# Block-sparse attention with a mixture of experts: score matmuls that read neighbouring and outer key blocks straight from the keys' tile

## The chip, the cores and the metric

The kernel runs on one core of a Trainium2 chip, with float32 data. The metric is the device time of one execution in microseconds (us), and the median of the runs counts. TensorE (PE) does the matmuls, VectorE (DVE) reductions and transposes, ScalarE (ACT) exponentials and copies, GpSimd (POOL) copies, and SyncE (SP) issues DMAs. SBUF is the on-chip memory that all of them read, PSUM the memory that matmuls write.

## The reference, cut to what matters

Attention over 4 batches of 8 heads, 768 positions of 64 features, in 24 blocks of 32 positions. A query block sees its own block, its two neighbours, blocks 0 and 23, and three sampled blocks; query blocks 0 and 23 see all. The result goes through a layer of 8 experts with 4 slots each.

```python
scores = scale * np.matmul(q, k.transpose(0, 1, 3, 2))
mask = np.abs(blk_i - blk_j) <= window            # window = 1
mask = mask | (blk_i == 0) | (blk_j == 0) | (blk_i == n_blocks - 1) | (blk_j == n_blocks - 1)
for qb in range(n_blocks):
    for kb in sampled_blocks[qb]:
        mask[qb * block:(qb + 1) * block, kb * block:(kb + 1) * block] = True
...
attn = np.exp(scores - np.max(scores, axis=-1, keepdims=True))
attn = attn / (np.sum(attn, axis=-1, keepdims=True) + 1e-09)
out = np.matmul(attn, v)
...
logits = x @ phi      # x: (3072, 512), phi: (512, 32)
# slots: softmax of logits over the rows, times x; two expert layers w1, w2; combine: softmax over the slots
```

## The kernel before, in words

**Layout.** For a batch, the keys lie in one tile, `ktile`, transposed: 128 partitions are two heads of 64 features each, then 4 such head pairs, then 768 positions. Queries lie the same way in `q`, loaded for two query blocks at a time and scaled. One score matmul takes 64 partitions (one head) of 32 queries as weights and streams key columns past them; its output is a 32-partition strip of a PSUM tile `s` of 2 query blocks by 256 columns. So 8 tiles of TensorE's array (2 halves of rows, 4 strips of columns) work at a time.

**A pair of query blocks** is `plan_pair` (L502). A batch has 11 pairs for blocks 1 to 22, and the dense blocks 0 and 23 apart (`plan_dense`, L700). For each of the pair's two blocks, `stage_k` (L429) collects the 8 visible key blocks side by side in a staging tile `kst` of 256 columns, one of four that take turns: `fixed` (L437) copies the three neighbours (L442) and, when the staging tile is new to this batch, blocks 0 and 23 (L440), on GpSimd; `sampled_` (L444) copies the three sampled blocks, on ScalarE (L448) or GpSimd (L450), at addresses read from a register. Then `qk` (L515) runs 2 x 4 x 2 = 16 matmuls of 256 columns (L521). VectorE takes the maximum (L538), ScalarE the exponential (L543), VectorE transposes 32 by 32 (L550). The value products (L615) take the transposed chunks as weights, and the values of sampled blocks from a staging tile `vrs` that GpSimd fills (L466). Chunk numbers, which are the column blocks of the scores, stand in `av_heads` (L628 and L653).

**Order.** A planner (`Plan`, L80) sets the order of each engine's instructions before the program runs: each task has engines that may run it with an estimated duration (`("PE", 1.08)` for the score matmuls), tasks that it depends on, rotating buffers that it takes, and a due time (`n`, the pair's number, plus an offset). Among tasks that could start about the same time on an engine, the one with the least `turn` goes first. `turn` is the due time plus an entry of a table that is indexed by the order in which the kinds of task, told apart by their function's first line, were first added:

```python
kind = self.kinds.setdefault(f.__code__.co_firstlineno, len(self.kinds))
t.turn = key + BEHIND.get(kind, 0.0)
BEHIND = {17: 1.1, 23: -2.5, 24: 2.8, 37: -1.2, 46: 1.0, 70: 1.8, 71: -1.2}
```

`fixed` is kind 19, `sampled_` 20, the pair's score matmuls 21, maxima 22, exponentials 23, transposes 24, value staging 25. Kind 17 is the dense rows' exponential; 37 copies transposed rows out, 38 is the gate's logits, 46 the slot sums, 47 their accumulation; 70 normalises the combine weights, 71 and 72 split them in two terms.

**Weights.** 64 tiles of 512 KB. `NPRE` of them go into tiles of their own during attention, 12 into buffers that the last batch leaves free, and at the end of attention 9 more into the last batch's keys' and values' buffers, and `NLB` into the room that the staging tiles leave, plus 2 (`LORD`, L59, is the order of the last two groups). The rest are loaded when a used tile is free.

Of the kernel before, what the change touches and what calls it, by code (L numbers as in the profile page):

```python
# [11 lines left out]
F32 = mybir.dt.float32  # L12
I32 = mybir.dt.int32
F32R = mybir.dt.float32r
AF = mybir.ActivationFunctionType
# [5 lines left out]
BLK, NB, NR = 32, 24, 3  # L21
P = 128
NP = 4
# [14 lines left out]
NKST, NVR, NQ = 4, 6, 4  # L38
# [13 lines left out]
EH = NE // PW  # L52
OG = 4 // PW
TG = 512 // CW
NPRE, NLB = 11, 10
KW = {"ktile": 3, "v0": 6, "v1": 6, "ptd": 3}


LORD = [0, 1, 2, 3, 4, 5, -1, -2, -3, -4, 6, 7, 8, 9, -5, -6, 10, 11]  # L59
LCOLS = [slice(c, c + LC) for c in range(0, WP, LC)]  # L60
H1, HALF = 3, 4
CPES = [0, 0, 3, 3, 3, 2, 0, 0]
# [17 lines left out]
class Plan:  # L80
# [6 lines left out]
    def add(self, f, opts, deps, key, acq=(), byte=0, pre=None, pace=False):  # L87
        t = Task(f, opts if isinstance(opts, list) else [opts], deps, key, acq, byte, pre, pace)
        kind = self.kinds.setdefault(f.__code__.co_firstlineno, len(self.kinds))
        t.turn = key + BEHIND.get(kind, 0.0)  # L90
        self.tasks.append(t)
        return t
# [96 lines left out]
def attn_moe_kernel(ctx, tc, qT, kT, vfull, vtab, sampled, phi, w1, w2, out):  # L189
# [107 lines left out]
    pst = att.enter_context(tc.tile_pool(name="pst", bufs=1))  # L297
# [1 line left out]
    ktile, vtile = [None] * B, [None] * B  # L299

    ptd = [ptdb[:, r * NB * 2 * BLK:(r + 1) * NB * 2 * BLK].rearrange("p (k j q) -> p k j q", k=NB, j=2) for r in range(2)]
    kst = [pst.tile([P, NP, 256], F32, name=f"kst{n}") for n in range(NKST)]
    qst = [pst.tile([P, NP, 2, BLK], F32, name=f"q{n}") for n in range(NQ)]

    vrs = [None] * NVR
# [77 lines left out]
    use = []  # L383
# [40 lines left out]
        v_use[b].append(t_v[b])  # L424


    fresh, nst, nvs = {}, [0], [0]

    def stage_k(b, i, n, use):  # L429
        k = nst[0] % NKST  # L430
        nst[0] += 1
        st, new = kst[k], fresh.get(k) != b
        fresh[k] = b

        w, r0 = (0, 96) if i % 2 else (32, 0)

        def fixed(t):  # L437
            kv = ktile[b]
            if new:
                POOL.tensor_copy(out=st[:, :, 128:192].rearrange("p c (g s) -> p c g s", g=2),  # L440
                                 in_=kv.rearrange("p c (g s) -> p c g s", g=NB)[:, :, 0:NB:NB - 1, :])
            POOL.tensor_copy(out=st[:, :, w:w + 96], in_=kv[:, :, (i - 1) * BLK:(i + 2) * BLK])  # L442

        def sampled_(t):  # L444
            for j, o in enumerate((r0, 192, 224)):
                src = ktile[b][:, :, ds(t.vals[j] * BLK, BLK)]
                if t.eng == "ACT":
                    ACT.activation(out=st[:, :, o:o + BLK], in_=src, func=AF.Copy, scale=1.0)  # L448
                else:
                    POOL.tensor_copy(out=st[:, :, o:o + BLK], in_=src)  # L450

        f = add(fixed, ("POOL", 0.82 if new else 0.47), [t_k[b]], n - 4, acq=[("kst", use)])
        r = add(sampled_, [("ACT", 0.62), ("POOL", 0.73)], [f, t_sreg], n - 2.5,
                pre=lambda e: block_numbers(sreg, i, e, NB - 1))
        k_use[b].extend([f, r])
        use.extend([f, r])
        return st, r

    def stage_v(b, i, n, use):
# [42 lines left out]
    def plan_pair(b, g, n):  # L502
        T = tile_of(b, (g + 1) // 2)
        w = 1 if g and g % 2 == 0 else 0
        u = Rec()
        u.g = g
        kd, ku = [], []
        for r in range(2):
            use = []
            kd.append(stage_k(b, 2 * g + 1 + r, n, use))  # L510
            ku.append(use)
        t_q, q_use = plan_q(u, b, g + 1, n)
        s_use = [[], []]

        def qk(t):  # L515
            u.s = [psA.tile([P, 2, 256], F32, tag="s", name="s", bufs=SB) for _ in range(2)]
            for j in range(2):
                for p in range(NP):
                    for r in range(2):
                        s_ = slice(64 * r, 64 * r + 64)  # L520
                        PE.matmul(u.s[r][32 * p:32 * p + 32, j, :], lhsT=u.q[s_, p, j, :],  # L521
                                  rhs=kd[j][0][s_, p, :], start=True, stop=True)

        t_qk = add(qk, ("PE", 1.08), [t_q] + [k for _, k in kd], n, acq=[("s", s_use[0]), ("s", s_use[1])])
        qks[n] = t_qk
        q_use.append(t_qk)
        for use in ku:
            use.append(t_qk)
        u.p = [None] * 2
        if not T.turned:  # L530
            T.pt = [None] * 2
            T.n_pt = nt[0]
            nt[0] += 2
        for r in range(2):
            def top(t, r=r):
                u.nm = getattr(u, "nm", {})
                u.nm[r] = pw.tile([P, 2], F32, tag="nm", name="nm", bufs=4)
                DVE.tensor_reduce(out=u.nm[r], in_=u.s[r], axis=AX.X, op=ALU.max, negate=True)  # L538

            def exp(t, r, j):  # L540
                if j == 0:
                    u.p[r] = pw.tile([P, 2, 256], F32, tag="p", name="p", bufs=PB)
                ACT.activation(out=u.p[r][:, j, :], in_=u.s[r][:, j, :], func=AF.Exp,  # L543
                               bias=u.nm[r][:, j:j + 1], scale=1.0)


            def turn(t, r=r):
                if w == 0:
                    T.pt[r] = pw.tile([P, 8, 4, BLK], F32, tag=f"ptt{(T.n_pt + r) % PTB}", name="ptt", bufs=1)
                DVE.transpose(out=T.pt[r][:, :, 2 * w:2 * w + 2, :].rearrange("p k j q -> p j k q"),  # L550
                              in_=u.p[r].rearrange("p j (k q) -> p j k q", k=8))

            t_m = add(top, ("DVE", 0.6), [t_qk], n + 0.1 + 0.01 * r)
            p_use = []
            t_e = []
            for j in range(2):
                t_e.append(add(lambda t, r=r, j=j, exp=exp: exp(t, r, j), ("ACT", 0.37), [t_m] + t_e, n + 0.2 + 0.01 * r,
                               acq=[("p", p_use)] if j == 0 else []))
            s_use[r].append(t_e[1])
            acq = []  # L560
            if w == 0:
                T.pt_use = getattr(T, "pt_use", {})
                T.pt_use[r] = []
                acq = [("ptt", T.pt_use[r])]
            t_t = add(turn, ("DVE", 0.64), [t_e[1]] + ([T.turned[r]] if w else []), n + 0.3 + 0.01 * r, acq=acq)
            p_use.append(t_t)
            T.turned.append(t_t)
        u.vst = []
        for r in range(2):
            use = []  # L570
            v, t_s = stage_v(b, 2 * g + 1 + r, n, use)
            u.vst.append(v)
            T.staged.append(t_s)
            T.use.append(use)
        T.units.append(u)
        if g == 0 or w:
            plan_av(T, n)
# [45 lines left out]
    def av_heads(T, rs_):  # L623

        vt, us = vtile[T.b], T.units
        one = len(us) == 1
        m = 64 * len(us)
        for n, c in enumerate((4, 5)):  # L628
            for r in rs_:
                for g, s_ in G2:  # L630
                    av_mm(T.av, 64 * r if one else 0, m, g, r, T.pt[r][s_, c, 0:m // BLK].rearrange("p j q -> p (j q)"),
                          vt[s_, :, VPOS((0, NB - 1)[n]), r, :], n == 0, False)
        for c in (1, 2):
            for w, u in enumerate(us):
                for r in rs_:
                    for g, s_ in G2:
                        av_mm(T.av, 64 * r if one else 64 * w, 64, g, r,
                              T.pt[r][s_, c, 2 * w:2 * w + 2].rearrange("p j q -> p (j q)"),
                              vt[s_, :, VPOS(2 * u.g + c), r, :], False, False)
        for n in range(NR + 1):  # L640
            for w, u in enumerate(us):
                for r in rs_:
                    for j in range(2):
                        i = 2 * u.g + 1 + j
                        for g, s_ in G2:
                            if n == 0:

                                k, c = (i - 1, 0) if j == 0 else (i + 1, 3)
                                if k in (0, NB - 1):
                                    continue  # L650
                                v_ = vt[s_, :, VPOS(k), r, :]
                            else:
                                c = ((3, 0)[j], 6, 7)[n - 1]  # L653
                                v_ = u.vst[j][s_, :, n - 1, r, :]
                            av_mm(T.av, (64 * r if one else 64 * w) + 32 * j, 32, g, r, T.pt[r][s_, c, 2 * w + j], v_,
                                  False, n == NR)
# [778 lines left out]
```

## Time and profile before

| | |
|---|---|
| median of 3 runs | 312.58 us (310.84 to 313.65) |
| span of the profiled execution, first to last instruction | 312.2 us |
| time of the profiled execution beyond its span | not recorded; the median is 0.4 us above the span |
| TensorE busy | 278.2 us, 7167 matmul passes and as many weight loads |
| VectorE, ScalarE, GpSimd busy | 216.2, 162.1, 185.2 us |
| mean granted TensorE clock | 0.979 |
| DMA | 63.62 MB, 204 GB/s over the span |

A float32 matmul is two passes in the profile, each with its weight load. The profile has a row for each group of instructions: line, engine, operation, the tiles written and read, count, busy time of the group, mean duration of one in ns, idle time of the engine just before them, and what ended most of that idle time. "issue" there means that the engine waited for nothing that the profile shows. PEld is TensorE's weight loading, which overlaps its matmuls. Instructions are themselves fetched by DMA, in queues of the kind "instruction".

### The profile page before, as it was taken

What the parts mean: (1) busy time and instruction counts of PE and PEld (TensorE: products, weight loads), DVE (VectorE), ACT (ScalarE), POOL (GpSimd) and SP (SyncE); (2) the same over time, 40 slices, a digit from 0 to 9 for tenths busy, and PEclk for the clock granted to TensorE, in tenths of its full rate; (3) what the DMA queues carried; (4) which work ended last, traced back from release to release, by engine and by line L of the source; (5) the groups of instructions that cost most, each with busy time, mean ns of one, the idle gap of its engine ahead of it and who ended that gap; (6) DMA issues with size and microseconds to landing.
All of it is one profiled execution on the core that took longest, in us unless ns stands there. A gap on an engine that the chain in (4) does not pass through costs nothing.

```text
span 312.2 us, 17614 instructions
## 1 busy us (share of the span) xinstructions
PE 278.2 (89%) x7167; PEld 191.7 (61%) x7167; DVE 216.2 (69%) x499; ACT 162.1 (52%) x492; POOL 185.2 (59%) x521
## 2 busy tenths in 40 slices
PE   7689888759999999999999999999999889999750
PEld 6148656536787666777677776877577763466340
DVE  4789967536899879789998778999897253103260
ACT  0766748443367867737667763866761241004250
POOL 2879499772667869958599994847958004000000
PEclk9899999997999999999999999999999999999996
DMA  7935766540045654024475511667779999999998
GB/s 246 399 115 161 208 192 195 152 115 4 19 146 168 196 168 143 7 74 146 138 199 150 141 37 56 154 186 220 207 206 298 354 367 363 413 406 405 391 335 271
DMA packets 33506, 63.62 MB, mean 204 GB/s; under 512 B 5521, under 2 KB 18962, under 8 KB 33426
## 3 DMA queue, kind: packets, MB, share of 16 engines
q1 hardware_dynamic: 33280, 62.37, 62.1%
q8 instruction: 56, 0.92, 1.3%
q14 instruction: 24, 0.20, 0.2%
q10 hardware_dynamic: 146, 0.13, 0.1%
HBM read 56.19 MB, written 6.29 MB: 200 GB/s over the span
## 4 chain that ended last, share of the span: by engine, by line
PE 55%; DVE 14%; DMA 12%; issue 5%; POOL 4%; POOLq 4%; ACT 2%; SPq 1%; ACTq 0%; DVEq 0%
PE av L615 22%; PE s L521 6%; DMA q<-in_qT_dram 5%; PE avd L615 5%; PE pf L1233 5%; PE sd L717 3%; PE pso L1241 3%; DMA w<-in_w_dram 3%; POOLq L347 3%; PE mxt L808 3%; DVE nm L538 3%; DVE ptt L550 2%; DMA v<-in_vfull_dram 2%; DVE x L610 2%; POOL vrs L466 2%
## 5 line engine op out<-in xcount | busy, mean ns | idle before, releaser
L466 POOL COPY vrs<-v 128x260 f32 x264 | 95.5, 407 | 27.1 <-PE av L615 18.3
L543 ACT ACTIVATE p<-s,nm 128x256 f32<-128x256 f32 x176 | 73.4, 479 | 18.8 <-DVE nm L538 15.1
L615 PE MATMUL av<-v,ptt 64*64 64x130 f32 (+2 forms) x1728 | 74.8, 285 | 0.0
L615 PEld LDWEIGHTS av<-v,ptt 64*64 64x64 f32 (+2 forms) x1728 | 50.0, 131 | 27.0 <-issue 19.0
L550 DVE STREAM_TRANSPOSE ptt<-p 128x512 f32<-128x512 f32 x88 | 57.3, 687 | 2.8 <-ACT p L543 2.7
L538 DVE TENSOR_REDUCE nm<-s 128x2 f32<-128x512 f32 x88 | 55.3, 680 | 5.6 <-PE s L521 5.3
L521 PE MATMUL s<-kst,q 64*32 64x256 f32 x1408 | 49.9, 384 | 8.4 <-POOL kst L450 4.9
L442 POOL COPY kst<-ktile 128x384 f32<-128x384 f32 x88 | 42.7, 510 | 13.9 <-PE s L521 12.6
L615 PE MATMUL av<-vrs,ptt 64*32 64x130 f32 x2112 | 47.3, 274 | 3.3 <-issue 3.2
L448 ACT ACTIVATE kst<-ktile 128x128 f32 x162 | 37.4, 304 | 11.0 <-PE s L521 8.4
L521 PEld LDWEIGHTS s<-kst,q 64*32 64x32 f32 x1408 | 28.8, 106 | 20.3 <-POOL kst L450 7.4
L615 PEld LDWEIGHTS av<-vrs,ptt 64*32 64x32 f32 x2112 | 35.6, 105 | 6.1 <-issue 6.0
L450 POOL COPY kst<-ktile 128x128 f32 x102 | 25.6, 296 | 0.6 <-ACT kst L448 0.4
L748 ACT ACTIVATE pd<-sd,nb 128x384 f32<-128x384 f32 x32 | 16.5, 579 | 16.9 <-DVE nb L743 16.4
L615 PE MATMUL avd<-v,ptd 64*64 64x130 f32 x768 | 23.6, 271 | 1.0 <-DVE ptd L752 0.7
L615 PEld LDWEIGHTS avd<-v,ptd 64*64 64x64 f32 x768 | 22.0, 132 | 3.2 <-PE s L521 1.5
L359 ACT COPY xT<-mxt 128x512 f32<-128x512 f32 (+1 forms) x22 | 12.4, 566 | 20.6 <-PE mxt L808 20.6
L485 POOL TENSOR_SCALAR q<-q 128x256 f32<-128x256 f32 x28 | 11.4, 409 | 15.0 <-DMA q<-in_qT_dram 14.8
L717 PE MATMUL sd<-ktile,q 64*32 64x384 f32 x256 | 19.4, 552 | 0.6 <-ACT p L543 0.4
L735 DVE TENSOR_REDUCE nm<-sd 128x1 f32<-128x384 f32 x32 | 16.4, 545 | 3.9 <-PE sd L717 3.9
L483 ACT ACTIVATE q<-q 128x256 f32<-128x256 f32 x20 | 8.3, 417 | 19.5 <-DMA q<-in_qT_dram 19.5
L608 DVE TENSOR_SCALAR rs<-av 128x8 f32<-128x8 f32 (+1 forms) x27 | 4.3, 158 | 19.8 <-PE av L615 19.8
(119 smaller groups left out, 290.2 us busy)
## 6 DMA issues: line engine op xcount, KB each, us to landing
w<-in_w_dram SPq DMA_DIRECT2D x17, 512.0 KB, 10.2
q<-in_qT_dram SPq DMA_DIRECT2D x47, 128.0 KB, 2.8
w<-in_w_dram SPq DMA_DIRECT2D x44, 128.0 KB, 3.6
out_dram<-ob SPq DMA_DIRECT2D x22, 256.0 KB, 4.5
ktile<-in_kT_dram SPq DMA_DIRECT2D x48, 96.0 KB, 2.7
v<-in_w_dram SPq DMA_DIRECT2D x8, 512.0 KB, 11.0
v<-in_w_dram SPq DMA_DIRECT2D x24, 128.0 KB, 3.5
w<-in_w_dram SPq DMA_DIRECT2D x12, 256.0 KB, 6.3
```

The lines of the kernel that those rows point to most:

```text
L442: POOL.tensor_copy(out=st[:, :, w:w + 96], in_=kv[:, :, (i - 1) * BLK:(i + 2) * BLK])
L448: ACT.activation(out=st[:, :, o:o + BLK], in_=src, func=AF.Copy, scale=1.0)
L450: POOL.tensor_copy(out=st[:, :, o:o + BLK], in_=src)
L466: POOL.tensor_copy(out=st[:, :, j:j + 1, :], in_=vf[:, :, ds(t.vals[j], 1), :])
L521: PE.matmul(u.s[r][32 * p:32 * p + 32, j, :], lhsT=u.q[s_, p, j, :], rhs=kd[j][0][s_, p, :], start=True, stop=True)
L538: DVE.tensor_reduce(out=u.nm[r], in_=u.s[r], axis=AX.X, op=ALU.max, negate=True)
L543: ACT.activation(out=u.p[r][:, j, :], in_=u.s[r][:, j, :], func=AF.Exp, bias=u.nm[r][:, j:j + 1], scale=1.0)
L550: DVE.transpose(out=T.pt[r][:, :, 2 * w:2 * w + 2, :].rearrange("p k j q -> p j k q"), in_=u.p[r].rearrange("p j (k q) -> p j k q", k=8))
L615: PE.matmul(av[:, r * 2 * D1:(r + 1) * 2 * D1].rearrange("p (a d) -> p a d", a=2), lhsT=lhsT, rhs=rhs, start=start, stop=stop)
L717: PE.matmul(u.s[r][k][32 * p:32 * p + 32, :], lhsT=T.dq.q[s_, p, j, :], rhs=kt[s_, p, 384 * k:384 * (k + 1)], start=True, stop=True)
L735: DVE.tensor_reduce(out=u.nm[r][:, k:k + 1], in_=u.s[r][k], axis=AX.X, op=ALU.max, negate=True)
L748: ACT.activation(out=u.p[r][k], in_=u.s[r][k], func=AF.Exp, bias=u.nb[r], scale=1.0)
```

## The change

Staging tiles shrink from 256 to 96 columns and hold the three sampled blocks alone; `fixed` is gone. The score matmul of 256 columns is cut up by where its keys lie. For the first block of a pair: 96 columns of the block and its neighbours and 64 of blocks 0 and 23, both straight from `ktile`, and 96 from the staging tile. For the second block, the sampled columns lie in two places of the score tile: 96 and 64 from `ktile`, 32 and 64 from the staging tile. Blocks 0 and 23 move from columns 128 to 192 to the last 64, so chunks 4 and 5 become 6 and 7 and the reverse. The score matmuls now depend on the keys' loads, and the key tile is held until they end. The staging tiles' room (4 x 160 columns x 4 head pairs x 4 bytes = 10240 bytes per partition) takes two weight tiles: `NPRE` goes from 11 to 13, and `NLB` from 10 to 8. Since `fixed` is no longer a kind of task, every kind behind it has a number one lower; the table `BEHIND` is as it was.

```diff
-NPRE, NLB = 11, 10
+NPRE, NLB = 13, 8
...
-LORD = [0, 1, 2, 3, 4, 5, -1, -2, -3, -4, 6, 7, 8, 9, -5, -6, 10, 11]
+LORD = [0, 1, 2, 3, 4, 5, -1, -2, -3, -4, 6, 7, -5, -6, 8, 9]
...
-    kst = [pst.tile([P, NP, 256], F32, name=f"kst{n}") for n in range(NKST)]
+    kst = [pst.tile([P, NP, NR * BLK], F32, name=f"kst{n}") for n in range(NKST)]
...
     def stage_k(b, i, n, use):
-        k = nst[0] % NKST
+        st = kst[nst[0] % NKST]
         nst[0] += 1
-        st, new = kst[k], fresh.get(k) != b
-        fresh[k] = b
-        w, r0 = (0, 96) if i % 2 else (32, 0)
-        def fixed(t):
-            kv = ktile[b]
-            if new:
-                POOL.tensor_copy(out=st[:, :, 128:192].rearrange("p c (g s) -> p c g s", g=2),
-                                 in_=kv.rearrange("p c (g s) -> p c g s", g=NB)[:, :, 0:NB:NB - 1, :])
-            POOL.tensor_copy(out=st[:, :, w:w + 96], in_=kv[:, :, (i - 1) * BLK:(i + 2) * BLK])
 
         def sampled_(t):
-            for j, o in enumerate((r0, 192, 224)):
-                src = ktile[b][:, :, ds(t.vals[j] * BLK, BLK)]
+            for j in range(NR):
+                src, to = ktile[b][:, :, ds(t.vals[j] * BLK, BLK)], st[:, :, j * BLK:(j + 1) * BLK]
...
-        f = add(fixed, ("POOL", 0.82 if new else 0.47), [t_k[b]], n - 4, acq=[("kst", use)])
-        r = add(sampled_, [("ACT", 0.62), ("POOL", 0.73)], [f, t_sreg], n - 2.5,
+        r = add(sampled_, [("ACT", 0.62), ("POOL", 0.73)], [t_k[b], t_sreg], n - 2.5, acq=[("kst", use)],
                 pre=lambda e: block_numbers(sreg, i, e, NB - 1))
...
         def qk(t):
             u.s = [psA.tile([P, 2, 256], F32, tag="s", name="s", bufs=SB) for _ in range(2)]
+            kt = ktile[b]
+            own = kt[:, :, 2 * g * BLK:(2 * g + 4) * BLK]
+            ends = kt.rearrange("p c (g s) -> p c g s", g=NB)[:, :, 0:NB:NB - 1, :]
             for j in range(2):
-                for p in range(NP):
-                    for r in range(2):
-                        s_ = slice(64 * r, 64 * r + 64)
-                        PE.matmul(u.s[r][32 * p:32 * p + 32, j, :], lhsT=u.q[s_, p, j, :],
-                                  rhs=kd[j][0][s_, p, :], start=True, stop=True)
+                st, W = kd[j][0], slice(32 * j, 32 * j + 96)
+                parts = [(W, own[:, :, W]), (slice(192, 256), ends)]
+                parts += [(slice(96, 192), st)] if j == 0 else [(slice(0, 32), st[:, :, 0:32]), (slice(128, 192), st[:, :, 32:96])]
+                for o, k in parts:
+                    for p in range(NP):
+                        for r in range(2):
+                            s_ = slice(64 * r, 64 * r + 64)
+                            PE.matmul(u.s[r][32 * p:32 * p + 32, j, o], lhsT=u.q[s_, p, j, :], rhs=k[s_, p],
+                                      start=True, stop=True)
...
-        t_qk = add(qk, ("PE", 1.08), [t_q] + [k for _, k in kd], n, acq=[("s", s_use[0]), ("s", s_use[1])])
+        t_qk = add(qk, ("PE", 1.12), [t_q, t_k[b]] + [k for _, k in kd], n, acq=[("s", s_use[0]), ("s", s_use[1])])
         qks[n] = t_qk
+        k_use[b].append(t_qk)
...
-        for n, c in enumerate((4, 5)):
+        for n, c in enumerate((6, 7)):
...
-                                c = ((3, 0)[j], 6, 7)[n - 1]
+                                c = ((3, 0)[j], 4, 5)[n - 1]
```

More of the change, by code (lines that the diff above doesn't have):

```diff
@@ L424, in plan_loads @@
         v_use[b].append(t_v[b])
-    fresh, nst, nvs = {}, [0], [0]
+    nst, nvs = [0], [0]
     def stage_k(b, i, n, use):
-        k = nst[0] % NKST
+        st = kst[nst[0] % NKST]
         nst[0] += 1
-        st, new = kst[k], fresh.get(k) != b
-        fresh[k] = b
-        w, r0 = (0, 96) if i % 2 else (32, 0)
-        def fixed(t):
-            kv = ktile[b]
-            if new:
-                POOL.tensor_copy(out=st[:, :, 128:192].rearrange("p c (g s) -> p c g s", g=2),
-                                 in_=kv.rearrange("p c (g s) -> p c g s", g=NB)[:, :, 0:NB:NB - 1, :])
-            POOL.tensor_copy(out=st[:, :, w:w + 96], in_=kv[:, :, (i - 1) * BLK:(i + 2) * BLK])
         def sampled_(t):
-            for j, o in enumerate((r0, 192, 224)):
-                src = ktile[b][:, :, ds(t.vals[j] * BLK, BLK)]
+            for j in range(NR):
+                src, to = ktile[b][:, :, ds(t.vals[j] * BLK, BLK)], st[:, :, j * BLK:(j + 1) * BLK]
                 if t.eng == "ACT":
-                    ACT.activation(out=st[:, :, o:o + BLK], in_=src, func=AF.Copy, scale=1.0)
+                    ACT.activation(out=to, in_=src, func=AF.Copy, scale=1.0)
                 else:
-                    POOL.tensor_copy(out=st[:, :, o:o + BLK], in_=src)
-        f = add(fixed, ("POOL", 0.82 if new else 0.47), [t_k[b]], n - 4, acq=[("kst", use)])
-        r = add(sampled_, [("ACT", 0.62), ("POOL", 0.73)], [f, t_sreg], n - 2.5,
+                    POOL.tensor_copy(out=to, in_=src)
+        r = add(sampled_, [("ACT", 0.62), ("POOL", 0.73)], [t_k[b], t_sreg], n - 2.5, acq=[("kst", use)],
                 pre=lambda e: block_numbers(sreg, i, e, NB - 1))
-        k_use[b].extend([f, r])
-        use.extend([f, r])
+        k_use[b].append(r)
+        use.append(r)
         return st, r
```

## The prediction, made before the changed kernel ran

> **What bounds the kernel now.** I read the page first, then the stretches of the span, then the time line of TensorE's weight loads around its stalls, and the DMA view in narrow windows.
>
> ```profile
> span 312.2 us, 17614 instructions
> PE 278.2 (89%) x7167; PEld 191.7 (61%) x7167; DVE 216.2 (69%) x499; ACT 162.1 (52%) x492; POOL 185.2 (59%) x521
> ...
> q8 instruction: 56, 0.92, 1.3%
> ...
> PE 55%; DVE 14%; DMA 12%; issue 5%; POOL 4%; POOLq 4%; ACT 2%; SPq 1%; ACTq 0%; DVEq 0%
> ...
> L521 PE MATMUL s<-kst,q 64*32 64x256 f32 x1408 | 49.9, 384 | 8.4 <-POOL kst L450 4.9
> L442 POOL COPY kst<-ktile 128x384 f32<-128x384 f32 x88 | 42.7, 510 | 13.9 <-PE s L521 12.6
> ```
>
> TensorE is busy 89% of the span and holds 55% of the chain that ended last; no other engine comes near. The stretches split the span at 238.4 us: attention before it, the expert layers behind it.
>
> ```profile
> 14.00:238.40 224.40, 210.42 (x6343) 151.33 (x6328) 186.95 (x405) 139.57 (x435) 169.97 (x481) 0.99 0.51 144
> 238.40:312.20 73.80, 58.48 (x743) 34.13 (x742) 21.29 (x67) 17.29 (x42) 8.15 (x18) 0.96 0.99 365
> ```
>
> In attention TensorE is busy 210 of 224 us at full clock and the DMA engines are half idle; afterwards the DMA share is 0.99, so the expert layers are limited by weights arriving. The change adds TensorE instructions to the first part, so I asked what limits TensorE there. Here are weight loads on the time line, with the idle time before them in brackets:
>
> ```profile
> 100.35 0.79 PEld L615 LDWEIGHTS av<-vrs,ptt 64*32 64x32 f32 x48
> ...
> 106.57 0.41 PEld L615 LDWEIGHTS av<-vrs,ptt 64*32 64x32 f32 x31 [0.44 <-issue]
> ...
> 110.57 0.38 PEld L615 LDWEIGHTS av<-vrs,ptt 64*32 64x32 f32 x23 [0.51 <-issue]
> ```
>
> Two of these rows begin after a stall in the middle of one uniform group of matmuls, with no tile to wait for; the end of the group of 48 shows a third:
>
> ```profile
> 101.57 0.27 PE L615 MATMUL av<-vrs,ptt 64*32 64x130 f32 x1 [0.17 <-issue]
> ```
>
> They end at 101.57, 106.57 and 110.57. Counting between them gives the reason. The columns of the next two rows are window, length, then busy time and count for PE, PEld, DVE, ACT and POOL; the third row is TensorE's semaphore instructions in the first window.
>
> ```profile
> 101.56:106.56 5.00, 4.83 (x126) 3.29 (x125) 4.85 (x10) 3.88 (x12) 4.32 (x13) 1.00 0.62 187
> 106.56:110.56 4.00, 3.76 (x128) 2.79 (x128) 2.03 (x5) 3.88 (x16) 2.16 (x6) 1.00 0.57 169
> ...
> L521 PEldq EVENT_SEMAPHORE  x5: 51/51/278, 101.6 to 102.6; - x5
> ```
>
> 126+125+5 = 256 and 128+128 = 256. The stalls lie exactly 256 TensorE instructions apart. And 0.92 MB in 56 packets is 16.4 KB each, for 14334 matmuls and weight loads: 256 instructions of 64 bytes. Queue q8 fetches TensorE's code, one packet per 256 instructions. Four windows of the DMA view, 101.56 to 105.31, 105.4 to 107.9, 107.9 to 109.2 and 109.2 to 111.9 us, show when. The first and third hold one q8 packet each:
>
> ```profile
> q8 instruction: 1, 0.02, 1.8%
> ...
> q8 instruction: 1, 0.02, 6.0%
> ```
>
> the second and fourth hold none. So a block had landed by 105.3 and TensorE went on at 106.57; the next was fetched only after that, from 107.9, had landed by 109.2, and TensorE went on at 110.57. One block is fetched at a time, only after TensorE has entered the block before it, and is usable about 1.3 us after it lands. The cycle is 4.00 us per 256 instructions. Two more stretches that end in such a stall, and the fastest two blocks that I found:
>
> ```profile
> 158.25:166.30 8.05, 7.74 (x254) 5.70 (x254) 7.31 (x16) 6.34 (x19) 7.66 (x24) 1.00 0.73 203
> 166.30:174.12 7.82, 7.60 (x254) 5.59 (x255) 5.85 (x11) 5.89 (x20) 7.56 (x22) 1.00 0.44 127
> ...
> 141.61:148.95 7.34, 7.33 (x251) 6.59 (x255) 6.76 (x13) 4.96 (x18) 5.13 (x16) 1.00 0.48 150
> ```
>
> Each holds two blocks: 4.02, 3.91 and 3.67 us per block. Over all of attention:
>
> ```profile
> q8 instruction: 50, 0.82, 1.6%
> ```
>
> 50 blocks in 224.4 us, 4.49 us each. Attention already runs within 12% of the rate at which TensorE's code arrives. The busy share hides that: of a stall of half a microsecond, the last matmul's own 0.27 us (mean ns in the first row below) counts as busy.
>
> ```profile
> L615 PE MATMUL av<-vrs,ptt 64*32 64x130 f32 x2112 | 47.3, 274 | 3.3 <-issue 3.2
> ...
> L615 PEld LDWEIGHTS av<-vrs,ptt 64*32 64x32 f32 x2112 | 35.6, 105 | 6.1 <-issue 6.0
> ```
>
> **The matmuls.** Now a pair of query blocks has 16 score matmuls (2 blocks, 4 head pairs, 2 halves); 44 pairs make 704, and the profile shows 1408: each float32 matmul is two passes, each a weight load and a matmul, so four instructions. After the change a pair has 3 parts for one block and 4 for the other, 7 x 8 = 56 matmuls. That is 40 more, 160 more instructions per pair, 7040 over 44 pairs: 27.5 more blocks. Attention then has 77.5 blocks. At the pace between stalls, (4.00 + 8.05 + 7.82) / 5 = 3.97 us, they take 307.7 us, against 224.4 now: **+83.3 us**. Bounds: 3.67 us gives 284.4, or +60; today's average of 4.49, with all its other waits kept, gives 348.0, or +123.6. I take 3.97, since the added instructions turn most of today's other waits into time during which code is late anyway, while some blocks (the dense rows, transposes) will still exceed it.
>
> The matmuls themselves would not fit the old time even with code at hand. The score matmuls of two pairs stand on the time line as
>
> ```profile
> 101.80 2.08 PE L521 MATMUL s<-kst,q 64*32 64x256 f32 x64
> ```
>
> (2.08 - 0.38, one matmul's mean) / 63 = 27 ns per pass, 0.87 us for a pair's 32 passes. The tightest sustained pace of passes on the same 64x32 tiles is the row of 48 loads above: (0.79 - 0.105, one load's mean) / 47 = 14.6 ns. 112 passes at that pace are 1.64 us: +0.77 a pair, +33.8 us in all. This is no second term: 224 instructions at 3.97 us per 256 already last 3.47 us, and the passes run inside that. It is the price if code were never late.
>
> The Trainium skill speaks against my main term. "Runtime: NRT & Kernel Launch", section "Instruction fetch mechanics", says that code comes in 16 KiB blocks of 256 instructions, as here, but that the fetch is hidden, because the sequencer issues at about 20 cycles per instruction, more slowly than blocks arrive. By the trace, passes of two instructions follow each other at 14.6 ns, so 256 are issued in 1.87 us, under half of the 4.00 between two stalls. By the rule the sum would lack the 83.3 and hold 33.8 instead; I keep it as a rival.
>
> **The copies that go.** GpSimd loses the 88 copies of neighbours (42.7 us) and the 16 of outer blocks (L440):
>
> ```profile
> L440 POOL COPY kst<-ktile 128x256 f32<-128x256 f32 x16 | 6.5, 405 | 2.9 <-DMA ktile<-in_kT_dram 2.9
> ```
>
> 49.2 of its 185.2 us. On the path this is worth only what TensorE waits for staging, 4.9 us in the L521 row. When code is late for every block, that wait ends before the code arrives, so I count it at 0 inside the 83.3; without that cover it is -4.9.
>
> **Waits.** The score matmuls now wait for the key tile's DMAs directly; the copy that they waited for did so already: 0. They also hold the key tile until they end. The next batch but one reuses it, a batch later: 0. The same holds for the last batch, whose tile takes three weight tiles issued after the last score matmul as before. What queues behind the waiting score matmuls on TensorE is the value product of the tile before, which waits for later work anyway.
>
> **Weights.** Two more tiles of 512 KB are fetched during attention and two fewer at its end. Eight more issues on SP's queue and 1 MB at a DMA share of 0.51 lie beside attention: 0. At the end the engines are full:
>
> ```profile
> 256.00:285.00 29.00, 28.62 (x339) 13.35 (x338) 7.06 (x28) 3.78 (x10) 3.58 (x6) 1.00 1.02 396
> ```
>
> 1.05 MB at 396 GB/s is **-2.6 us**; bounds -2.6 and 0, if the end is set by something else.
>
> **The order.** The planner's offsets are looked up by the order in which task kinds first appear. With one kind gone, those of the pairs move: the hurry of -2.5 goes from exponentials to transposes, the delay of 2.8 from transposes to value staging. The products on TensorE need all three. VectorE, ScalarE and GpSimd have 37 to 85 idle us each in attention and will have some 80 more, so 0; if that cover is gone, up to 4.9 us, the size of TensorE's present waits for staging. Renumbering the chunks in the value product costs nothing: same instructions.
>
> **Sum.** 312.2 + 83.3 - 2.6 = 392.9 us of span. The span of the profiled execution is 0.4 us under the runs' median of 312.58, so **393 us**.
>
> **Rivals.**
> *Code is never late* (fetched further ahead once TensorE's stream is dense). Then the passes' own pace counts: 312.6 + 33.8 - 4.9 - 2.6 = 339 us. For it: the mean of 4.49 us lies above the cycle, so code was in time for many blocks. Against it: the stalls that I followed end about 1.3 us after a landing. Chance 0.09. The skill's rule above, were it true, would end here.
> *Not slower: the columns decide.* Each tile still streams 256 key columns per query block. If passes of 96, 64 and 32 columns are issued at the pace of their columns, which takes 224 instructions in the present 1.04 us of a pair (4.6 ns each) or less, the score matmuls cost what they do now, GpSimd's copies leave the path (-4.9) and the end gains 2.6: 305 us. For it: loads within one burst start closer than 14.6 ns. Against it: no 48 of them do, and the 256-instruction stalls. Chance 0.06.
> *Code arrives more slowly still.* One block took 5.00 us (first stretch above), perhaps behind other transfers. At 4.49 us, the present mean, the time is 312.6 + 123.6 - 2.6 = 434 us. For it: the DMA share was 0.62 there. Against it: the same bytes spread over a longer time. Chance 0.07.
>
> **How the numbers follow.** My forecast has 0.78. Its own range is 370 (3.67 us per block) to 428 (4.40). The whole range begins a little lower, at 360, for a cycle that shortens once less data competes, and ends at 428; the first two rivals and most of the third lie outside, about 0.2. A measurement here tells 1%, 3 us, from no change, since three runs of the same kernel spread over 2.8 us. Faster by over 1%: 0.06, the second rival. Within 1%: 0.02, if part of it is eaten up. Slower: 0.92.
>
> **What would show it.** L521 should have 4928 matmuls, q8 some 83 or 84 packets, with 77 or 78 in attention, and attention should end near 320 us. TensorE should stall for "issue" at nearly each 256th instruction, mostly within score matmuls, with 3.7 to 4.2 us per block; GpSimd should have some 136 busy us. It is wrong if blocks pass in under 3.4 us, if stalls name other engines, or if q8 has two packets between two stalls. The matmul's own price shows where code is at hand: some 15 ns per pass if I am right, 8 (27 x 73 / 256, at a mean of 73 columns) if columns decide.

## The result, and the profile after

The changed kernel took 397.35 us (median of 4 runs, 391.57 to 399.06) against 313.12 us for the kernel before (310.84 to 313.72): a ratio of 1.260, 95% interval 1.248 to 1.272. Medians here count all executions, while ratios compare only those in the faster of the two states into which executions of a kernel fall, so the two can differ by a per cent. The profiled execution took 396.32 us, 1.8 us more than its span.

The page of the changed kernel, in the lines that answer to those of before:

```profile
span 394.5 us, 24582 instructions
PE 314.1 (80%) x10687; PEld 236.6 (60%) x10687; DVE 217.7 (55%) x502; ACT 167.1 (42%) x505; POOL 138.0 (35%) x401
...
q8 instruction: 84, 1.38, 1.5%
...
PE 69%; issue 15%; DMA 8%; DVE 3%; ACT 2%; SPq 0%; ACTq 0%; DVEq 0%
...
L516 PE MATMUL s<-ktile,q 64*32 64x64 f32 (+1 forms) x2816 | 61.9, 244 | 31.0 <-issue 25.5
...
L516 PE MATMUL s<-kst,q 64*32 64x64 f32 (+2 forms) x2112 | 53.7, 233 | 20.8 <-issue 20.8
```

The score matmuls are 2816 + 2112 = 4928 passes where there were 1408, and the code is 84 packets where it was 56. GpSimd's work fell from 185.2 to 138.0 us, and the time did not gain by it. "issue", a wait for nothing that the profile shows, grew from 5% to 15% of the chain that ended last, and most of the score matmuls' idle time (25.5 + 20.8 of 51.8 us) is of that kind. Before, most of it was a wait for staging: 4.9 of 8.4 us ended with L450, the copy of the sampled blocks.

Where the 82.3 us went is shown by the first expert matmul in the chain of waits. Before it stood at 256.46:

```profile
256.46 6.22 PE pf L1233 x56
```

and after:

```profile
339.98 6.22 PE pf L1229 x56
```

So attention became 83.5 us longer, and the rest, 55.7 us before, took 54.5. The stretches of the changed kernel and the code packets in the first of them:

```profile
13.00:322.00 309.00, 247.81 (x9875) 196.47 (x9860) 190.82 (x414) 145.32 (x450) 128.24 (x374) 0.94 0.39 116
322.00:394.50 72.50, 58.16 (x740) 34.45 (x739) 20.16 (x64) 17.28 (x42) 6.39 (x13) 0.95 0.91 334
```

```profile
q8 instruction: 78, 1.28, 1.8%
```

309.0 / 78 = 3.96 us per block of 256 instructions, and TensorE is now idle for 61 of the 309 us even by its busy share (14 of 224 before). One block can be followed on the time line. These are the first and last matmul rows of a block and the first of the next, with the stretches of this block and the next, counted as before:

```profile
22.60 0.35 PE L516 MATMUL s<-ktile,q 64*32 64x96 f32 x16 [1.31 <-issue]
...
23.73 0.51 PE L516 MATMUL s<-ktile,q 64*32 64x96 f32 x25
26.33 0.25 PE L516 MATMUL s<-ktile,q 64*32 64x64 f32 x2 [2.10 <-issue]
```

```profile
22.59:26.31 3.72, 1.63 (x128) 1.47 (x128) 2.10 (x6) 1.80 (x7) 2.65 (x9) 1.00 0.25 57
26.31:30.27 3.96, 3.41 (x127) 3.08 (x127) 3.29 (x6) 2.71 (x7) 2.90 (x9) 1.00 0.32 95
```

The first window holds 128 matmul passes and 128 weight loads, one block to the instruction. They start between 22.60 and 24.00 (the last row ends at 24.24, less the 0.24 that one pass takes): 1.40 us for 127 steps, 11 ns a pass. Then TensorE stands still until 26.33. In the DMA view one q8 packet lies in 22.59 to 25.13 us, none in 25.13 to 27.68, and the next in 27.68 to 28.93:

```profile
q8 instruction: 1, 0.02, 3.5%
...
q8 instruction: 1, 0.02, 6.2%
```

It is the pattern of the kernel before, now at most blocks: TensorE goes on 1.2 us after the packet's window ends, and the next packet comes only after that.

The whole trace bears it out. Count TensorE's instructions (matmuls, weight loads and semaphores, in order of their start) in steps of 256, with 22.60 us as one of the steps. From 15 to 321 us, the pauses before every 256th instruction add up to 73.7 us; with the count begun at any other of the 255 places, they come to at most 2.4 us. 53 of the 77 blocks begin after a pause of over 0.1 us, and each of these begins 1.2 to 1.6 us after the end of its packet. They begin 3.85 us after the block before, on average; the other 24, whose code was there in time, 4.26 us.

### The profile page after: what moved, and what is told of

Read it like the earlier page. It is cut to its first block, busy times and chain, and to the rows that moved or that the text cites. A ratio compares the mean times of both kernels' runs of the same rounds, so it can differ in the third digit from the quotient of the medians.

```text
span 394.5 us, 24582 instructions
## 1 busy us (share of the span) xinstructions
PE 314.1 (80%) x10687; PEld 236.6 (60%) x10687; DVE 217.7 (55%) x502; ACT 167.1 (42%) x505; POOL 138.0 (35%) x401
## 4 chain that ended last, share of the span: by engine, by line
PE 69%; issue 15%; DMA 8%; DVE 3%; ACT 2%; SPq 0%; ACTq 0%; DVEq 0%
PE av L611 29%; PE s L516 17%; PE avd L611 6%; PE mxt L804 4%; PE pf L1229 4%; DMA kw<-in_w_dram 3%; DMA v<-in_w_dram 3%; PE sd L713 2%; PE ml L839 2%; PE ms L889 2%; DMA ktile<-in_kT_dram 1%; PE st L381 1%; DVE nm L534 1%; PE po L1333 1%; DMA q<-in_qT_dram 1%
## 5 line engine op out<-in xcount | busy, mean ns | idle before, releaser
L516 PE MATMUL s<-ktile,q 64*32 64x64 f32 (+1 forms) x2816 | 61.9, 244 | 31.0 <-issue 25.5
L611 PE MATMUL av<-v,ptt 64*64 64x130 f32 (+2 forms) x1728 | 82.8, 304 | 3.8 <-issue 3.7
L437 ACT ACTIVATE kst<-ktile 128x128 f32 x180 | 42.4, 299 | 80.0 <-PE s L516 77.4
L611 PEld LDWEIGHTS av<-v,ptt 64*64 64x64 f32 (+2 forms) x1728 | 54.5, 140 | 31.4 <-issue 23.7
L516 PEld LDWEIGHTS s<-ktile,q 64*32 64x32 f32 x2816 | 47.3, 109 | 38.4 <-issue 36.5
L516 PE MATMUL s<-kst,q 64*32 64x64 f32 (+2 forms) x2112 | 53.7, 233 | 20.8 <-issue 20.8
L516 PEld LDWEIGHTS s<-kst,q 64*32 64x32 f32 x2112 | 36.2, 108 | 23.1 <-issue 23.1
L439 POOL COPY kst<-ktile 128x128 f32 x84 | 21.4, 293 | 59.9 <-PE s L516 48.4
L611 PEld LDWEIGHTS av<-vrs,ptt 64*32 64x32 f32 x2112 | 39.0, 113 | 5.6 <-issue 5.6
L359 ACT COPY xT<-mxt 128x512 f32<-128x512 f32 (+1 forms) x19 | 10.7, 565 | 41.8 <-PE mxt L804 41.8
L804 PE MATMUL mxt<-ident,x 128*128 128x128 f32 x96 | 17.8, 309 | 1.5 <-DVE x L593 1.0
```

The lines of the kernel that those rows point to most:

```text
L437: ACT.activation(out=to, in_=src, func=AF.Copy, scale=1.0)
L439: POOL.tensor_copy(out=to, in_=src)
L516: PE.matmul(u.s[r][32 * p:32 * p + 32, j, o], lhsT=u.q[s_, p, j, :], rhs=k[s_, p], start=True, stop=True)
L611: PE.matmul(av[:, r * 2 * D1:(r + 1) * 2 * D1].rearrange("p (a d) -> p a d", a=2), lhsT=lhsT, rhs=rhs, start=start, stop=stop)
L804: PE.transpose(T.px[:, c, :], T.x[:, c * P:(c + 1) * P], ident)
```

## The experiments

The theory is that TensorE's code sets the pace: 256 instructions per 3.7 to 4.2 us, whatever they do. Rival A is that passes are issued at their own pace and code is never late; rival B that columns decide, or that the cost lies in reading the keys' tile, in the missing copies or the new waits; rival C that the planner's moved offsets carry part of the loss. Times of each kernel are compared with runs of the kernel before on the same chip, whose medians were 314.88, 313.9 and 316.2 us in the three groups.

**The same code without the columns, and half of it (x1_tiny40, x2_tiny20).** To the kernel before, after its 8 score matmuls of each query block:

```diff
+                for d in range(20):          # 10 in x2_tiny20
+                    p, r = d % NP, d // NP % 2
+                    s_ = slice(64 * r, 64 * r + 64)
+                    PE.matmul(u.s[r][32 * p:32 * p + 32, j, 0:1], lhsT=u.q[s_, p, j, :],
+                              rhs=kd[j][0][s_, p, 0:1], start=True, stop=True)
```

> The kernel before, with 40 more score matmuls of one single column per pair of query blocks, which write column 0 again with the value it has: as many instructions for TensorE as the changed kernel (84 packets of code), next to no columns, all copies kept. Theory (code arrives one block of 256 instructions per 3.97 us): 388 to 402 us, with over 60 us of 'issue' waits. Rival A (passes issue at 14.6 ns, code never late): 80 more passes per pair are 1.17 us, 44 pairs 51 us, so 364 us. Rival B (columns decide, or it is the reading from the keys' tile or the missing copies that cost): 312 to 318 us.

> The same with 20 such matmuls per pair: half of the added instructions, 3520, 13.75 blocks. Theory: attention has 63.75 blocks; at 3.97 us each that is 253 us, 29 more than before, and up to half of the full dose, 42, where blocks still wait for other things: 342 to 355 us. Rival A: half of 51, 338 us. Rival B: 312 to 316 us.

Measured: 405.13 us (ratio 1.290, 1.282 to 1.299) and 353.23 us (1.120, 1.111 to 1.128). Forty matmuls of one column cost a little more than cutting the real ones up did; rival A's 364 and rival B's 318 are far off. The half dose lies where the theory put it. The full dose came out 3 us above the top of the theory's range, and the "issue" waits of its matmuls in attention add up to 41.8 us, not to over 60; the pauses before every 256th instruction, counted as above, are 51.9 us, fewer than the 73.7 of the changed kernel, since its own passes fill more of each block (272.7 us busy in attention against 245.5). A row of its one-column passes:

```profile
106.71 0.57 PE L526 MATMUL s<-kst,q 64*32 64x1 f32 x38
```

With 0.17 us for one pass, (0.57 - 0.17) / 37 = 10.8 ns each, the pace of the passes of 32 to 96 columns above. So a pass on these tiles costs 11 ns with one column as with 32 to 96, and 128 of them 1.4 us: far from the 3.85 us between blocks. At this pace, in place of 14.6 ns, rival A would give 351 us for the full dose and not 364.

**The cut alone (x3_cut_staged).** The kernel before with all staging, but:

```diff
-                for p in range(NP):
+                cuts = [0, 96, 160, 256] if j == 0 else [0, 96, 160, 192, 256]
+                for lo, hi in zip(cuts, cuts[1:]):
+                    for p in range(NP):
...
+                            PE.matmul(u.s[r][32 * p:32 * p + 32, j, lo:hi], lhsT=u.q[s_, p, j, :],
+                                      rhs=kd[j][0][s_, p, lo:hi], start=True, stop=True)
```

> The kernel before with all its staging copies, weights and order, only its score matmuls cut into the same widths as in the changed kernel (96, 64, 96 and 96, 64, 32, 64), all reading the staging tile. Theory: the cut alone costs what the change cost, so 396 to 402 us, the changed kernel's 397 plus 0 to 3 for the two weight tiles. Rival B (the direct reading, the missing copies or the new waits cost): near 313 us. Rival A: 347 us, 313 + 34.

Measured: 401.54 us, ratio 1.277 (1.269 to 1.286). The cut costs all that the change cost; rival B falls with it. The pauses before every 256th instruction add up to 76.4 us here, and to at most 2.1 us at any other place of the count. The whole of GpSimd's copies (187.4 us busy here, 138.0 in the changed kernel) hides behind it.

**A smaller cut (x7_five_parts).** In the changed kernel, blocks 0 and 23 are staged again behind the sampled ones:

```diff
...
-                parts = [(W, own[:, :, W]), (slice(192, 256), ends)]
-                parts += [(slice(96, 192), st)] if j == 0 else [(slice(0, 32), st[:, :, 0:32]), (slice(128, 192), st[:, :, 32:96])]
+                parts = [(W, own[:, :, W])]
+                parts += [(slice(96, 256), st)] if j == 0 else [(slice(0, 32), st[:, :, 0:32]), (slice(128, 256), st[:, :, 32:160])]
```

> The changed kernel with blocks 0 and 23 staged again behind the sampled ones, once per staging tile and batch, so that a pair has 5 parts (96, 160 and 96, 32, 128 columns), 40 matmuls in place of 56; weights as before. 4224 more instructions than before, 16.5 blocks. Theory: at the 2.8 us per added block that the half dose showed, and the 3.1 that the change showed, 46 to 51 us more: 357 to 368 us. Rival A (14.6 ns per pass, code never late): 80 passes are 1.17 us, 0.30 more than now, 13 us in all: 326 us.

Measured: 361.61 us, ratio 1.161 (1.148 to 1.174), inside the theory's range and 36 us above rival A's.

**Fewer instructions than before (x8_wide512).** One matmul of 512 columns for two of 256; the second query block's scores are left out:

```diff
-            for j in range(2):
...
+                    PE.matmul(u.s[r][32 * p:32 * p + 32], lhsT=u.q[s_, p, 0, :],
+                              rhs=kd[0][0][s_, p, :].unsqueeze(1).to_broadcast([64, 2, 256]), start=True, stop=True)
```

> The kernel before with half of the score matmuls at twice the columns: the first query block of a pair streams its staged keys into both halves of the score tile, 8 matmuls of 512 columns in place of 16 of 256. It leaves out the second block's scores. The same columns, 1408 instructions less, 5.5 blocks. Theory: the kernel before is itself limited by code in part, so 2.8 to 4.0 us per block are gained: 291 to 300 us. Rival (columns and TensorE's busy time set the pace of before): 310 to 316 us.

Measured: 310.85 us, ratio 0.991 (0.983 to 0.998). The theory's number fell here: 5.5 blocks less are worth 3 us (0.6 to 5 by the interval), not 14 to 23. In the window 14.0 to 235.7 us this kernel has 44 code packets and this row:

```profile
14.00:235.70 221.70, 210.60 (x5663) 137.60 (x5648) 186.47 (x408) 140.11 (x436) 169.31 (x481) 0.97 0.52 146
```

221.7 / 44 = 5.04 us per block, well above the cycle of code, and TensorE is busy 210.6 us, as long as before (210.4). So what held the kernel before was mostly TensorE's own passes and its turns with the other engines, and code was late for some blocks only. The two limits lay close, and a block takes the longer one. So the price of a block is no constant: in the medians of each group, 0.6 us for the 5.5 blocks taken away (3.1 us), 2.8 for the first 13.75 added (38.4 us), 2.9 for 16.5 (47.7 us), and 3.1 to 3.3 for all 27.5 (84.2, 86.7 and 90.3 us for the change, the cut alone and the single columns). The last half alone costs 3.3 to 3.8, near the cycle. TensorE's granted clock in attention falls along the same row (0.98 in x2, 0.97 in x7, 0.94 in the cut alone, 0.90 with the single columns), so a part of the rise may be the clock's; no run separates the two.

**The order (x4_order, x5_after_order, x12_order_again).** The offsets moved in the kernel before, and moved back in the changed one:

```diff
-BEHIND = {17: 1.1, 23: -2.5, 24: 2.8, 37: -1.2, 46: 1.0, 70: 1.8, 71: -1.2}
+BEHIND = {17: 1.1, 24: -2.5, 25: 2.8, 38: -1.2, 47: 1.0, 71: 1.8, 72: -1.2}   # before: x4
+BEHIND = {17: 1.1, 22: -2.5, 23: 2.8, 36: -1.2, 45: 1.0, 69: 1.8, 70: -1.2}   # changed: x5, x12
```

> The kernel before with the planner's offsets moved to the task kinds that have them in the changed kernel, nothing else. Theory: the engines that are reordered have room, so 309 to 317 us, within about 1% of before. Rival C (the moved offsets carry a good part of the 84 us): over 325 us.

> The changed kernel with the planner's offsets moved back to the task kinds that had them before. Theory: TensorE's code sets the pace, so the order of the other engines matters little: 391 to 400 us, against 397 for the changed kernel. Rival C (the moved offsets carry part of the loss): under 389 us.

> The changed kernel with the planner's offsets at their old task kinds, beside the changed kernel on the same chip. Theory: within 1% of it (4 us). Rival C (the moved offsets cost): 4 us or more faster. If the moved offsets suit this kernel better, slower by 4 us or more.

**The weights (x6_after_weights, x13_weights_again)**, beside the changed kernel again (x11_after_again):

```diff
-NPRE, NLB = 13, 8
+NPRE, NLB = 11, 10
...
-LORD = [0, 1, 2, 3, 4, 5, -1, -2, -3, -4, 6, 7, -5, -6, 8, 9]
+LORD = [0, 1, 2, 3, 4, 5, -1, -2, -3, -4, 6, 7, 8, 9, -5, -6, 10, 11]
```

> The changed kernel with the weights as before (11 tiles early, 10 late). Theory: 1.05 MB more at the end at 396 GB/s, 2.6 us: 398 to 402 us. Rival (the end is set by something else): 395 to 398 us.

> The changed kernel again, so that the next two are compared with it on one chip: a ratio to before of 1.25 to 1.28.

> The changed kernel with 11 weight tiles early and 10 late, beside the changed kernel on the same chip. Theory: 2.6 us slower; in the first look the stretch from the first expert matmul to the end was 56.7 us in place of 54.6, which is 2.1. Rival (the two tiles do more than their bytes): 6 us or more.

| kernel | median us | ratio to before, 95% interval |
|---|---|---|
| x4_order (before, offsets moved) | 320.94 | 1.009 (1.003 to 1.015) |
| x5_after_order | 400.76 | 1.283 (1.268 to 1.298) |
| x11_after_again | 402.90 | 1.274 (1.256 to 1.293) |
| x12_order_again | 400.30 | 1.279 (1.268 to 1.290) |
| x6_after_weights | 404.17 | 1.298 (1.284 to 1.313) |
| x13_weights_again | 403.59 | 1.287 (1.277 to 1.297) |

In the kernel before the moved offsets cost 0.9%, about 3 us. In the changed kernel their effect lies within the intervals, and rival C has no part of the 84 us worth the name. x5 and x6 came out above what the theory gave them (400 and 402), but so did the changed kernel itself on a later chip (402.9), so these two said little alone. Beside it, old weights made 0.7 us of median and 0.013 of ratio, and the intervals overlap: a cost of 1 to 4 us in the changed kernel is likely, its size is not settled. The profile of x6 points the same way. Its first expert matmul stands at

```profile
343.88 6.21 PE pf L1229 x56
```

in a span of 400.5, so 56.6 us remain there, against 54.5 in the changed kernel: 2.1 us. But the end does not follow the number of late tiles alone. In x3, which has as many late tiles as before and x6, the first expert matmul stands at

```profile
344.95 6.21 PE pf L1235 x56
```

in a span of 397.6, which leaves 52.7 us: less than in the changed kernel. What the two tiles are worth by themselves is not shown.

**The part that helps, alone (x10_three_stages).** The kernel before with three staging tiles in place of four, and the room used for one early weight tile:

```diff
-NKST, NVR, NQ = 4, 6, 4
+NKST, NVR, NQ = 3, 6, 4
...
-NPRE, NLB = 11, 10
+NPRE, NLB = 12, 9
...
-LORD = [0, 1, 2, 3, 4, 5, -1, -2, -3, -4, 6, 7, 8, 9, -5, -6, 10, 11]
+LORD = [0, 1, 2, 3, 4, 5, -1, -2, -3, -4, 6, 7, 8, -5, -6, 9, 10]
```

> The kernel before with three staging tiles for keys in place of four; the room takes one more weight tile early (12) and one fewer late (9). It takes the one part of the change that helps, without added instructions. 0.52 MB fewer at the end are 1.3 us; if three staging tiles hold TensorE up, up to 5 us are lost. Theory: 308 to 318 us, at best 1% under before.

Measured: 331.30 us, ratio 1.056 (1.045 to 1.067), much worse than expected. From its page:

```profile
L521 PE MATMUL s<-kst,q 64*32 64x256 f32 x1408 | 56.0, 384 | 14.9 <-POOL kst L442 6.0
```

and from the instructions of that line, weight loads included, the first of what TensorE sat idle for, with times and counts:

```profile
POOL kst L442: 16.8, 19
```

The kernel before has in that place:

```profile
POOL kst L442: 1.3, 1
```

A pair takes two staging tiles, so three of them leave the next pair half staged: the score matmuls wait for the neighbours' copies, and GpSimd's idle time before these copies, ended by the score matmuls of a pair before, grew from 12.6 to 22.2 us. That the 15 us come from this is read from the waits; the one weight tile that moved as well was not tried apart. No kernel here beats the one before by more than the 1% of x8, which leaves out work.

## Why the prediction was right

- *What bounds the kernel now.* Code arriving as the limit, and its cycle, were read rightly: the profile after has 3.96 us per block where 3.97 was taken. But 3.96 is a mean of two kinds: steps that end in a pause for code (3.85 us), and 24 of 77 that end without one, in which TensorE was held by its own work or other waits (4.26 us). The prediction named the second kind and gave it no number. What was said of before, that attention runs "within 12%" of that rate, is true of the mean, but x8 shows that code was not what held most blocks; the prediction drew no number from taking code away, so this did not hurt it.
- *The matmuls.* 27.5 blocks foretold, 28 packets more measured; +83.3 us foretold, +83.5 to the first expert matmul. That these agree to 0.2 us is luck: executions of the changed kernel lie between 391.6 and 399.1 us, and the two kinds of step evened out. x3 shows that the cut alone does it, x1 that added passes of one column do it as well.
- *The price of a pass.* 14.6 ns was too much: 11 ns in the changed kernel and in x1. It is neither of the two paces named as signs, 15 ns and 8 ns; what tells the theories apart is the pause behind the passes. With code never late, 112 passes would be 1.23 us, not 1.64, and the first rival would have given 16 us rather than 33.8. The row of 48 loads held passes of 130 columns, which have a pace of their own, so it was a bound and not the price. No part of the sum hung on it.
- *The skill's rule.* The Trainium skill ("Runtime: NRT & Kernel Launch", section "Instruction fetch mechanics") has the fetch hidden behind issue at some 20 cycles per instruction. The trace disagrees: 256 instructions were issued in 1.40 us and waited 2.3 us for the next block. Another page would have given nearly the same total for another reason: the Trainium skill ("TensorE: Matmul & The Clock Gate", section "Back-to-back issue gap") has a floor of about 25 ns from start to start for matmuls of 1 to 64 columns. An estimate from that figure, taken for all 112 passes: 2.80 us, 1.93 more than before and 85 us over 44 pairs. Only the pace inside a block, 11 ns, and the stall behind it tell the two apart.
- *The copies that go.* 0 inside the sum; right, since x3 with all copies is as slow to about 1%. The 4.9 us named as their price without that cover ended with L450, the copy of the sampled blocks, which stays; what the neighbours' copies before it had in this wait was not shown.
- *Waits and order.* 0 foretold. In the changed kernel the order's effect is below 1%, in the kernel before 0.9%, within the 4.9 us given as the price without cover.
- *Weights.* -2.6 foretold; the end is 1.2 us shorter than before, and 2.1 shorter than with the old weights in one profile. Between runs it isn't resolved, and x3 has a still shorter end with the old weights, so this term is not shown.
- *The sum.* 392.9 us of span foretold, 394.5 measured. The time lies 1.8 us over the span, where 0.4 was taken from the median of other runs. The top of the range, 428 us, belongs to 4.42 us per block; the 4.40 written beside it gives 427.

Rivals: "code is never late" and "the columns decide" fell with x1 and x3. "Code arrives more slowly still" fell too: the mean cycle was 3.96 us, not 4.49.

## What to carry to other kernels

Count TensorE's instructions, not only its columns: a float32 matmul here is four, and here 256 of them came 3.85 us apart where TensorE waited for them, while small passes needed 1.4 us to run. In this kernel both limits lay close, so 5.5 blocks of code taken away brought 0.6 us each, and the first 13.75 added cost 2.8 us each. Whether cutting one matmul into several at equal columns is free depends on whether its passes take longer than their code. To see it, look for "issue" stalls inside uniform groups and count the instructions between them.

## What the runs showed of the hardware beyond that

The mean granted clock of TensorE in attention fell from 0.99 to 0.94 in the changed kernel, and to 0.90 in x1 with its one-column passes:

```profile
14.00:329.00 315.00, 272.74 (x9728) 216.91 (x9718) 187.04 (x402) 142.73 (x435) 172.17 (x479) 0.90 0.38 110
```

In the changed kernel the lower clock lies mostly where code was in time: its mean was 0.86 in the steps of 256 instructions that end without a pause, and 0.99 in those that end with one. That waiting for code and narrow passes are counted as little work would fit this; no run here shows it. x1 took 3.6 us more than x3 at the same number of instructions, and the intervals of their ratios overlap; whether the clock or its own passes (256 and one column) had a part in it was not tried.
